# A linear-attention and FFN kernel: all steps of its first part in one table of places, in finer pieces, every place set anew

## Chip, core and metric

The kernel runs on one core of one Trainium2 chip. The metric is the device time in microseconds of one execution, the median over runs.

## What is computed

Two layers follow each other. In the first, each of 8 batches and 8 heads has q, k and v of 576 x 64 (fp32): kv = k^T v, out = q kv, an rms norm over the 64 columns with eps 1e-6, times a gain. The heads are laid side by side, which gives x of 4608 x 512. The second is a feed-forward layer without bias, with the mish function between two products:

```python
kv = np.einsum('bhsd,bhse->bhde', k, v)
out = np.einsum('bhsd,bhde->bhse', q, kv)
x = out / np.sqrt(np.mean(out * out, axis=-1, keepdims=True) + 1e-06) * g_norm
h = x @ w_in            # 4608 x 512 @ 512 x 2048
g = h * np.tanh(softplus(h))
return g @ w_out        # 2048 x 512
```

## The kernel before

The kernel has two parts. The first makes g and writes it to DRAM (gd, gp); the second reads g in blocks of 256 tokens and makes g @ w_out. The change touches the first part, in which w_out is also converted and written to DRAM (wod) for the second.

The 4608 tokens are nine tiles of 512, numbered j. For each tile the attention runs in two units u of four heads, and each unit is a chain of steps (function unit_steps): load (q from DRAM, SP), transpose (PE for tiles 0 and 1, DVE after), project (q times kv, PE), square (ACT), scaled (times the gain, ACT or DVE), sums (PE), rstd (ACT, with two table loads), keep (the rms row to DRAM, SP, line 418), spread (the row back from DRAM, broadcast over 64 partitions, SP, line 424), normalize (DVE, line 432). From tile 1 on the two units share sums, rstd and keep, under unit 1. The steps of kv are k.load (SP), k.mul (PE, line 266), k.keep (ACT).

All products are made in split precision: each operand is a hi half (an ACT copy that rounds, line 115) and a lo half (a DVE subtraction, line 116), and a product is three passes. The FFN of tile 0 is a plain product. From tile 1 on it is a Strassen-like scheme with seven products per 2 x 2 of blocks; the operands made from x are called forms (x_form: A11, S1, S2, S4, A12, S3, A22, in the table numbers 0 to 6), three of which need additions first. Tiles 1 and 2 run alone, tiles 3 to 8 in pairs. The weights have seven forms too; some stay in SBUF, the others are written to DRAM (wid) and streamed back for each group (stream, lines 193 and 194, SP).

The first part is laid out in slots. A slot is one product on PE: 6 matmuls in slots 0 to 31 (line 549), 12 narrow ones in slots 32 to 87 (line 571, slot 34 is empty, slot 90 is one of these), 6 in slots 88 to 255 (line 581). Seven slots are a group. A group opens bank "a" in its first slot; its second-last and last results are added up by DVE in the second, third and fourth slot after it has begun its last two products (line 616), and the last product of a group is made in the third slot of the next group, into the same bank "a", after the addition of block "22" has read it. ACT copies and applies mish to the results (lines 498, 503, 511, 112), GpSimd's queue stores them.

Every other step is put behind a slot by hand: at(t, f) appends f to the list of slot t, and the slot emits first its evictions, then its product, then its list, in the order of the calls. What runs before slot 0 stands in the code as it is emitted. Each engine executes its own instructions in the order of emission. start(j) is the first slot of tile j: 0, 32, 60, 88, 116, 144, 172, 200, 228.

Of the kernel before, what the change touches and what calls it, by code (L numbers as in the profile page):

```python
# [8 lines left out]
F32 = mybir.dt.float32  # L9
# [12 lines left out]
B12 = T4  # L22


@with_exitstack
def linear_attention_rms_mish_ffn(
# [432 lines left out]
    def x_form(j, f, added=False):  # L459
        a11, a12, a21, a22 = x_block(j, 0, 0), x_block(j, 1, 0), x_block(j, 0, 1), x_block(j, 1, 1)  # L460
        xs1 = x_s1(j)
        if f == S1 and not added:
# [5 lines left out]
        split(*x_at(j, f), {A11: a11, S1: xs1, S2: a11, A12: a12, S4: a12, S3: a21, A22: a22}[f])  # L468
# [9 lines left out]
    def at(t, f):  # L478
        plan.setdefault(t, []).append(f)
# [4 lines left out]
    def slot(t, product=None):  # L484
        for f in evict.pop(t, ()):
            f()
        if product:
            product()
        for f in plan.pop(t, ()):
            f()  # L490
# [166 lines left out]
    nc.scalar.preload_act_table_set("natural_log_exp_and_others")  # L657
    weights(0, LOAD)
    rows[0], turned_q = (wfp.tile([P, n, T], F32, name=f"wf{h}4") for n, h in ((TR, "b"), (2, "a")))
    for c in range(TR):  # L660
        rows_load(0, c, 0, 4)
    for name, n in (("k", 2), ("v", 3)):
        kv0[name] = wfp.tile([P, NKC - 1, 9 * D], F32, name=f"wfb{n}")
        kv0[name, NKC] = wfp.tile([P, 9 * D], F32, name=f"pc{n - 2}")
    kv_first(first)
    weights(1, LOAD)
    for c in range(TR):
        rows_load(0, c, 4, 4)
    kv_first(rest)
    for r in (slice(0, D), slice(D, P)):  # L670
        nc.gpsimd.dma_start(gcol[r, :], g_norm.rearrange("(p o) -> p o", o=1))
    weights(2, LOAD)
    weights(3, LOAD)
    make_identity(nc, ident)
    nc.gpsimd.memset(eps, 1e-6)
    nc.gpsimd.memset(ones, 0.0)
    nc.gpsimd.memset(ones[0:D, 0:D], 1.0)
    nc.gpsimd.memset(ones[D:P, D:P], 1.0)
    nc.gpsimd.memset(sel, 0.0)
    for o in range(2):  # L680
        nc.gpsimd.memset(sel[o * D:(o + 1) * D, o:o + 1], 1.0)

    weights(4, LOAD)
    k_load(1, 0)
    k_load(1, 1)

    weights(0, SCALE, JOIN)
    do(0, 0, "transpose", "turned")
    weights(0, BLOCKS)
    kv_first_product(first)  # L690
    kv_first_keep(first)
    weights(1, SCALE)
    do(0, 0, "project", "square")
    weights(1, JOIN)
    do(0, 1, "transpose")
    do(0, 0, "sums")
    do(0, 1, "turned")
    weights(1, BLOCKS)
    do(0, 0, "rstd")
    kv_first_product(rest)  # L700
    kv_first_keep(rest)
    do(0, 0, "normalize")
    do(0, 1, "project")
    weights(2, SCALE)
    x_whole(0)
    do(0, 1, "square")
    weights(3, SCALE)
    rows[1] = att.tile([P, TR, H * D], F32, name="qs")
    for c in range(TR):
        rows_load(1, c, 0, H)  # L710

    def first_slot():
        do(0, 1, "sums")
        weights(2, JOIN)
        do(0, 1, "rstd", "normalize")
# [24 lines left out]
    for b, t, loads, made in (  # L740
        (2, start(0), (21, 22, 23, 28), (27, t1 + 2)),
# [6 lines left out]
        for n in range(2):  # L748
            at(t + made[n], lambda b=b, n=n: k_product(b, n))
            at(t + made[n] + 1, lambda b=b, n=n: k_keep(b, n))  # L750
        for p in range(4):
            at(t + loads[p], lambda b=b, p=p: k_load(b, p))

    def attention(j, t, steps):
        def both():
            units[j][0]["spread"]()
            units[j][1]["spread"]()
        units[j][0]["both"] = both
        for u, n, *names in steps:
            at(t + n, lambda u=u, names=names: do(j, u, *names))  # L760
# [439 lines left out]
```

## Time and profile before

| | us |
|---|---|
| median of 3 runs | 868.23 |
| lowest, highest | 866.71, 868.54 |
| the profiled execution | 872.09 |
| its span, first to last instruction | 870.3 |

The rows below come from the profiled execution; times in them count from the start of its span. In a timeline row the first number is the start, the second the length, and in brackets stands how long the engine was idle before and what ended that. A name such as "ur<-a,ur" is the tile written and the tiles read. "SPq" is SP's queue, whose rows are issues of transfers. PEclk is the granted share of TensorE's clock.

### The profile page before, as it was taken

How to read it: one execution, taken by the hardware profiler on the slowest of the kernel's cores; microseconds unless marked ns; L12 is line 12 of the kernel's file. 1: busy time of each engine (PE TensorE's matmuls, PEld its weight loads, DVE VectorE, ACT ScalarE, POOL GpSimd, SP SyncE). 2: the span in 40 equal slices, each digit the busy share in tenths (PEclk: the TensorE clock that was granted, in tenths of full speed). 3: DMA queues.
4: the chain of work that ended last, by engine and by line, in shares of the span. 5: the costliest groups of instructions: out<-in, count | busy, mean ns of one | idle time of the engine just before them, and what ended most of it. 6: DMA issues, size and time to landing. Idle time of an engine off the chain costs nothing.

```text
span 870.3 us, 14063 instructions
## 1 busy us (share of the span) xinstructions
PE 799.6 (92%) x5456; PEld 666.0 (77%) x5456; DVE 580.8 (67%) x714; ACT 439.2 (50%) x639; POOL 104.1 (12%) x191
## 2 busy tenths in 40 slices
PE   5899899997998669788799999999999999999998
PEld 3677788796766547566688898888888888888887
DVE  3676745556464486454826368888878787888875
ACT  3766663764544354445546565444444445444452
POOL 1010412110222122222111110000000000000000
PEclk9999989998999989899999999999999999999999
DMA  9967887986998947877776764345344333444421
GB/s 279 300 232 249 291 315 237 291 247 216 309 317 287 283 152 244 259 273 248 283 239 237 264 220 158 121 147 168 122 159 132 121 121 121 129 148 131 154 69 49
DMA packets 118434, 181.09 MB, mean 208 GB/s; under 512 B 18720, under 2 KB 80160, under 8 KB 118368
## 3 DMA queue, kind: packets, MB, share of 16 engines
q1 hardware_dynamic: 102848, 128.74, 48.6%
q0 software_dynamic: 15424, 51.39, 15.5%
q8 instruction: 43, 0.70, 0.4%
q14 instruction: 23, 0.19, 0.1%
q10 hardware_dynamic: 96, 0.07, 0.0%
HBM read 119.21 MB, written 60.95 MB: 207 GB/s over the span
## 4 chain that ended last, share of the span: by engine, by line
PE 66%; DMA 15%; DVE 9%; ACT 4%; issue 3%; SPq 3%; POOL 0%; DVEq 0%; ACTq 0%; POOLq 0%
PE a L956 14%; PE bc L956 11%; PE a L581 10%; PE a L961 7%; PE bc L581 7%; PE bc L961 5%; DMA wfa<-wid 3%; DMA qs<-in_q_dram 3%; DMA fa<-rd 2%; PE a L571 2%; DMA wod<-w 2%; PE x L372 1%; PE bc L549 1%; PE a L549 1%; PE bc L571 1%
## 5 line engine op out<-in xcount | busy, mean ns | idle before, releaser
L112 ACT ACTIVATE ur<-ur 128x1024 f32<-128x1024 f32 x32 | 33.9, 1060 | 69.3 <-DVE ur L616 69.3
L581 PE MATMUL a<-pc,wfb 128*128 128x512 f32 x96 | 39.3, 452 | 28.1 <-DVE ur L616 28.1
L616 DVE TENSOR_TENSOR ula<-bc,ula 128x512 f32<-128x512 f32 x32 | 22.0, 688 | 62.9 <-PE bc L581 35.9
L581 PEld LDWEIGHTS a<-pc,wfb 128*128 128x128 f32 x96 | 20.7, 216 | 37.6 <-DVE ur L616 32.4
L581 PE MATMUL bc<-wfa,wfa 128*128 128x512 f32 x144 | 37.8, 399 | 7.9 <-DMA wfa<-wid 7.2
L581 PEld LDWEIGHTS bc<-wfa,wfa 128*128 128x128 f32 x144 | 26.8, 189 | 15.0 <-DVE wx L121 4.0
L511 ACT COPY ur<-a 128x512 f32<-128x512 f32 x32 | 18.8, 588 | 37.9 <-PE a L581 30.0
L581 PE MATMUL a<-wfc,wfc 128*128 128x512 f32 x96 | 37.3, 430 | 0.0
L581 PE MATMUL bc<-wfc,wfb 128*128 128x512 f32 x144 | 37.2, 394 | 0.0
L581 PE MATMUL a<-wfa,wfb 128*128 128x512 f32 x144 | 36.9, 392 | 0.0
L116 DVE TENSOR_TENSOR wfa<-g,wfa 128x1024 fp32r<-128x1024 f32 (+1 forms) x24 | 27.5, 1155 | 12.8 <-ACT wfa L115 12.8
L115 ACT CAST wfc<-wfb 128x1024 fp32r<-128x1024 f32 x23 | 24.0, 1051 | 20.9 <-PE a L961 7.8
L581 PE MATMUL bc<-pa,wfb 128*128 128x512 f32 x96 | 34.0, 395 | 0.0
L581 PE MATMUL a<-pb,wfa 128*128 128x512 f32 x96 | 33.6, 390 | 0.0
L115 ACT CAST wfa<-g 128x1024 fp32r<-128x1024 f32 (+1 forms) x24 | 23.8, 998 | 18.7 <-PE a L961 7.8
L581 PEld LDWEIGHTS bc<-wfc,wfb 128*128 128x128 f32 x144 | 27.3, 191 | 6.3 <-issue 0.3
L581 PEld LDWEIGHTS a<-wfa,wfb 128*128 128x128 f32 x144 | 26.7, 188 | 6.6 <-issue 1.0
L112 ACT ACTIVATE ula<-ula 128x512 f32<-128x512 f32 x32 | 20.2, 632 | 21.7 <-DVE ula L616 21.7
L115 ACT CAST wfa<-wfb 128x1024 fp32r<-128x1024 f32 x19 | 19.9, 1051 | 21.5 <-PE a L961 15.5
L116 DVE TENSOR_TENSOR wfa<-wfb,wfa 128x1024 fp32r<-128x1024 f32 x19 | 23.1, 1221 | 8.9 <-ACT wfa L115 8.9
L616 DVE TENSOR_TENSOR ur<-bc,ur 128x512 f32<-128x512 f32 x32 | 21.9, 683 | 10.5 <-PE bc L581 3.6
L1011 DVE TENSOR_TENSOR ur<-ow 128x1024 f32<-128x1024 f32 x16 | 19.6, 1224 | 13.1 <-ACT ow L1008 13.1
(516 smaller groups left out, 2460.1 us busy)
## 6 DMA issues: line engine op xcount, KB each, us to landing
gp<-ur POOLq DMA_DIRECT2D x24, 512.0 KB, 5.2
g<-gp SPq DMA_DIRECT2D x12, 1024.0 KB
wfb<-gp SPq DMA_DIRECT2D x12, 1024.0 KB
wfa<-wid SPq DMA_DIRECT2D x18, 512.0 KB
w<-in_moe_w_out_dram SPq DMA_DIRECT2D x32, 256.0 KB
km<-in_k_dram SPq DMA_DIRECT2D x28, 288.0 KB
vm<-in_v_dram SPq DMA_DIRECT2D x28, 288.0 KB
gp<-ula POOLq DMA_DIRECT2D x24, 256.0 KB, 4.2
```

The costliest lines, as they stand in the source:

```text
L112: nc.scalar.activation(o, i, AF.Mish)
L115: nc.scalar.copy(hi, src)
L116: nc.vector.tensor_sub(lo, src, hi.bitcast(F32))
L372: nc.tensor.matmul(st["x"][a][half(o), c], kv[r], st["q"][r, a, c], start=True, stop=True)
L511: then(t + 4, lambda: nc.scalar.copy(dst(st, "12"), st["a"]))
L549: nc.tensor.matmul(banks[m], w[:, a, kc, :], xf[b][:, kc], start=r == kc == s == 0, stop=(r == kc == 1 and s == 2), skip_group_check=True,)
L571: nc.tensor.matmul(bank[:, jj * TH:(jj + 1) * TH], w[:, a, kc, :], xf[b][:, kc], start=first and jj == kc == s == 0, stop=(kc == 1 and s = ...
L581: nc.tensor.matmul(bank, w[:, a, kc, :], xf[b][:, kc], start=first and kc == s == 0, stop=(kc == 1 and s == 2), skip_group_check=True,)
L616: nc.vector.tensor_add(o, bank_view(st, block, bank), o)
L956: nc.tensor.matmul(bank.rearrange("p (s h n) -> p s h n", s=2, h=2), gf[0][:, c], wo_form(c, right), start=first and c == 0, stop=False, s ...
L961: nc.tensor.matmul(halves(bank)[:, 0], gf[1][:, c], wo_form(c, right)[:, 0], start=False, stop=c == NF2 - 1, skip_group_check=True)
L1011: nc.vector.tensor_add(st["o"].rearrange("p r (c n) -> p (r c) n", c=2), a[:, :, 0], a[:, :, 1])
```

## The change

A table WHEN gives each of 485 steps of the first part a place, a number with three decimals; its whole part is the slot, and within a slot the steps are sorted by place. Steps before slot 0 have negative places. The finer pieces: a form is now its addition (f{j}.{f}.sum, DVE), its hi half (f{j}.{f}.0, ACT) and its lo half (f{j}.{f}.1, DVE), each with a place; the two spreads of a tile, each step of a unit, each step of a weight block (w{j}) and of a chunk of w_out (o{i}), the streams (s{i}.{n}), the loads and splits of the second part's weights (p{c}) and its early forms (e{c}.{f}) have one each. Instructions, transfers and tiles are the same; order and place differ. The diff, cut:

```diff
+WHEN = {
+    "w1.load": -57.761, "w1.scale": -57.665, "kv.a": -56.646, "rows.a": -56.517, "w0.load": -55.073, "kv.mul.a": -54.701,
...
+    "x0.1.square": -11.17, "x0.1.sums": -9.952, "w2.scale": -8.597, "w2.join": -6.356, "x0.1.rstd": -5.266,
...
+    "w2.blocks": -2.398, "w3.scale": -1.588, "k1.load2": 1.685, "k1.mul0": 2.528, "k1.keep0": 4.733, "w3.join": 5.805,
...
+    "k3.load0": 29.125, "x2.1.load": 29.175, "f1.0.1": 30.119, "w4.diff": 30.214, "k2.mul1": 30.411, "f1.2.sum": 30.523,
...
+    "x2.0.square": 31.886, "k3.load1": 31.947, "f1.4.0": 32.101, "f1.2.0": 32.737, "f1.4.1": 32.792, "f1.2.1": 33.196,
...
+    "x2.0.scaled": 39.667, "x2.1.project": 40.062, "x3.0.load": 40.076, "w5.sums": 40.306, "k3.mul0": 40.507,
...
+    "w4.store": 49.281, "x2.1.rstd": 49.741, "x2.1.keep": 50.313, "k3.keep1": 50.903, "x3.0.transpose": 51.079,
+    "w6.store": 51.568, "k4.load1": 51.698, "k4.mul0": 52.246, "w7.sums": 52.262, "x2.0.spread": 52.367,
+    "x2.0.normalize": 52.723, "x3.0.project": 52.826, "x2.1.spread": 53.018, "f2.0.0": 53.224, "pools.xt": 54.093,
...
+    "x3.1.normalize": 71.16, "x4.1.sums": 71.188, "x4.1.rstd": 72.176, "pools.wx": 72.928, "x4.1.scaled": 72.948,
+    "o0.load": 73.332, "o0.scale": 73.59, "x5.0.load": 73.996, "x4.1.keep": 74.235, "x3.0.spread": 74.587,
+    "o0.join": 75.149, "f3.4.0": 75.377, "x3.0.normalize": 75.565, "f3.0.0": 75.727, "x4.1.spread": 76.127,
...
+    "o0.store": 79.406, "x4.0.spread": 79.7, "x4.1.normalize": 80.724, "x4.0.normalize": 81.317, "k5.keep0": 81.319,
+    "k5.load3": 81.38, "k6.load0": 81.631, "k5.mul1": 82.565, "k6.load1": 82.703, "k5.keep1": 83.056, "f3.1.sum": 84.967,
+    "f3.2.sum": 85.423, "f3.1.0": 85.515, "x5.1.load": 85.681, "k6.load2": 85.804, "f3.2.0": 86.314, "f3.1.1": 86.495,
...
+    "x5.1.scaled": 103.717, "o4.load": 104.024, "x5.0.spread": 105.109, "s0.2": 105.184, "x5.1.spread": 105.458,
...
+    "k7.keep1": 122.327, "x6.1.sums": 122.642, "o6.load": 123.413, "x6.1.rstd": 123.617, "x6.1.keep": 124.487,
+    "s0.5": 124.541, "o6.scale": 126.126, "x6.0.spread": 126.594, "o6.join": 127.287, "o6.diff": 127.431,
+    "o6.store": 128.496, "x6.0.normalize": 131.613, "x6.1.spread": 132.132, "x7.0.transpose": 132.458, "o7.load": 133.0,
+    "x6.1.normalize": 133.011, "f5.1.sum": 133.652, "o7.scale": 134.666, "o7.join": 136.841, "f5.0.0": 137.267,
...
+    "o9.scale": 154.219, "o9.join": 155.712, "o10.load": 156.204, "o9.diff": 157.661, "x7.0.spread": 157.999,
+    "x7.0.normalize": 158.323, "x8.0.transpose": 158.502, "o9.store": 158.999, "o10.scale": 159.093, "s1.2": 160.404,
...
+    "o13.load": 176.057, "o13.scale": 176.556, "x8.1.rstd": 176.69, "o13.join": 176.923, "s1.4": 178.899,
+    "o13.diff": 179.328, "o13.store": 179.491, "o14.load": 180.623, "o14.scale": 181.143, "o14.join": 183.595,
+    "x8.1.keep": 183.886, "s1.5": 184.157, "o14.diff": 184.314, "o14.store": 184.554, "x8.0.spread": 185.555,
+    "x8.0.normalize": 186.509, "o15.load": 187.081, "x8.1.spread": 187.181, "x8.1.scaled": 188.636, "o15.scale": 189.095,
+    "o15.join": 190.662, "s1.6": 191.845, "x8.1.normalize": 193.314, "f7.1.sum": 193.614, "f7.0.0": 194.153,
+    "f7.0.1": 194.91, "f7.1.0": 197.56, "f7.2.sum": 197.819, "f7.1.1": 198.895, "f7.4.0": 199.888, "f7.2.0": 200.459,
...
+    "s2.4": 231.214, "p3.load": 232.696, "p2.load": 233.51, "e0.6": 234.071, "p1.split": 235.921, "p4.load": 236.909,
...
+    "e1.1": 249.971, "p5.load": 250.354, "p5.split": 250.686, "e1.0": 254.85,
+}
...
-    def x_form(j, f, added=False):
...
+    def x_sum(j, f):
+        a11, a12 = x_block(j, 0, 0), x_block(j, 1, 0)
+        if f == S1:
             x_add(j)
         elif f == S2:
-            nc.vector.tensor_sub(a11, xs1, a11)
+            nc.vector.tensor_sub(a11, x_s1(j), a11)
         elif f == S4:
             nc.vector.tensor_sub(a12, a12, a11)
...
+    def x_form(j, f, low):
...
+        if low:
+            nc.vector.tensor_sub(lo, src, hi.bitcast(F32))
+        else:
+            nc.scalar.copy(hi, src)
...
     def at(t, f):
-        plan.setdefault(t, []).append(f)
+        plan.setdefault(int(t // 1), []).append((t, f))
+
+    def step(name, t, f):
+        at(WHEN.get(name, t), f)
...
+    def steps(t):
+        for _, f in sorted(plan.pop(t, ()), key=lambda s: s[0]):
             f()
...
+    for t in sorted(t for t in plan if t < 0):
+        steps(t)
```

The places of the same steps before, where the text speaks of them: k3.load0 and k3.load1 32 and 35, k3.mul0 41, w7.sums 48, k4.load1 51, x2.1.rstd 49, x2's spreads 52 and normalizes 56 and 57, x3's spreads 72 and normalizes 76 and 77, x4's spreads 79 and normalizes 83 and 84, s0.2 102, x6's rstd 128, spreads 131 and normalizes 135 and 136, x7's spreads 163 and normalizes 167 and 168, x8.0.transpose 164, s1.4 172 (after o14.load, also 172), x8's spreads 187 and normalizes 191 and 192, p5.load 250 and p5.split 258. A hi half was directly followed by its lo half.

## Rows read from the trace of the kernel before

**Rows 1.** The page of the profiled execution, its first part: each engine's busy us, share of the span, and instructions.

```profile
PE 799.6 (92%) x5456; PEld 666.0 (77%) x5456; DVE 580.8 (67%) x714; ACT 439.2 (50%) x639; POOL 104.1 (12%) x191
```

**Rows 2.** Busy time of each engine in stretches that begin at the first matmul of slots 0, 32, 60, 88, 116, 144, 172, 200, 228 and 256. The columns: the stretch, its length, then for each engine the busy us and the number of instructions, the granted clock, the busy share of the 16 DMA engines, and what they moved in GB/s.

```profile
0.00:27.04 27.04, 15.73 (x181) 9.96 (x181) 10.17 (x11) 13.34 (x17) 2.68 (x15) 1.00 0.99 294
27.04:88.15 61.11, 58.22 (x469) 42.74 (x469) 43.88 (x58) 39.55 (x61) 6.52 (x12) 1.00 0.82 253
88.15:143.95 55.80, 50.03 (x580) 46.34 (x581) 31.12 (x50) 31.44 (x57) 16.84 (x29) 0.94 0.89 302
143.95:201.01 57.06, 53.99 (x706) 47.92 (x705) 34.49 (x41) 33.71 (x53) 7.94 (x12) 1.00 0.84 255
201.01:255.15 54.14, 48.24 (x376) 36.64 (x375) 29.17 (x40) 27.71 (x43) 10.54 (x18) 0.94 0.81 268
255.15:314.59 59.44, 46.69 (x337) 35.41 (x336) 33.09 (x51) 25.78 (x40) 15.59 (x27) 0.94 0.86 276
314.59:376.45 61.86, 48.94 (x218) 35.84 (x217) 36.86 (x57) 29.33 (x43) 15.59 (x27) 0.89 0.75 236
376.45:425.93 49.48, 43.57 (x186) 32.44 (x185) 28.93 (x44) 24.19 (x35) 13.77 (x24) 0.97 0.82 282
425.93:472.11 46.18, 41.21 (x170) 33.22 (x169) 24.13 (x32) 25.77 (x40) 6.60 (x13) 0.93 0.62 218
472.11:512.70 40.59, 40.59 (x191) 34.04 (x189) 18.69 (x34) 22.41 (x42) 6.92 (x13) 1.00 0.64 222
512.70:870.32 357.62, 352.35 (x2059) 311.41 (x2057) 290.27 (x303) 166.00 (x215) 1.08 (x2) 1.00 0.42 133
```

**Rows 3.** The timeline of PE: the matmuls in front of which PE stood for 1.5 us or more between slot 0 and slot 256. They are in slots 41, 90, 117, 124, 139, 146, 160, 167, 174, 180 and 202.

```profile
110.41 0.37 PE L266 MATMUL ss<-vm,km 64*64 64x64 f32 x2 [4.18 <-DMA vm<-in_v_dram]
...
210.79 2.93 PE L571 MATMUL a<-pd,wfb 128*128 128x256 f32 x12 [5.62 <-DVE ur L616]
...
259.45 1.63 PE L581 MATMUL bc<-wfa,wfa 128*128 128x512 f32 x6 [1.57 <-DMA wfa<-wid]
...
272.53 1.62 PE L581 MATMUL bc<-wfa,wfa 128*128 128x512 f32 x6 [2.03 <-DMA wfa<-wid]
...
305.82 0.79 PE L581 MATMUL a<-pc,wfb 128*128 128x512 f32 x1 [7.52 <-DVE ur L616]
...
325.31 0.79 PE L581 MATMUL a<-pc,wfb 128*128 128x512 f32 x1 [6.58 <-DVE ur L616]
...
352.21 0.50 PE L581 MATMUL a<-pc,wfb 128*128 128x512 f32 x1 [2.98 <-DVE ur L616]
...
365.71 0.80 PE L581 MATMUL a<-pc,wfb 128*128 128x512 f32 x1 [3.36 <-DVE ur L616]
...
380.85 0.50 PE L581 MATMUL a<-pc,wfb 128*128 128x512 f32 x1 [1.52 <-DVE ur L616]
...
394.31 2.22 PE L581 MATMUL bc<-wfa,wfa 128*128 128x512 f32 x6 [3.57 <-DMA wfa<-wid]
...
434.07 0.80 PE L581 MATMUL a<-pc,wfb 128*128 128x512 f32 x1 [4.20 <-DVE ur L616]
```

**Rows 4.** The chain of work that ended last, in order of time: two consecutive slots each (start, length, count of matmuls).

```profile
325.31 5.29 PE a L581 x12
...
434.07 5.49 PE a L581 x12
...
474.99 2.72 PE a L581 x12
```

**Rows 5.** The timeline of DVE ahead of slots 139 and 202, with the addition of line 616 that PE waited for (305.08), and an instruction of a join of w_out, a form's first addition and lo halves (lines 122, 456, 116) for their lengths.

```profile
299.98 1.23 DVE L432 TENSOR_TENSOR wfa<-wfa,fh 128x1024 f32<-128x1024 f32 x1 [6.34 <-DMA fh<-rd]
...
302.15 1.23 DVE L432 TENSOR_TENSOR wfa<-wfa,fa 128x1024 f32<-128x1024 f32 x1 [0.34 <-DMA fa<-rd]
...
303.75 0.69 DVE L122 SCALAR_TENSOR_TENSOR wx<-w,wx 128x512 uint32<-128x512 uint32 x1
...
305.08 0.68 DVE L616 TENSOR_TENSOR ur<-a,ur 128x512 f32<-128x512 f32 x1
...
306.84 1.18 DVE L456 TENSOR_TENSOR s<-wfa,wfa 128x1024 f32<-128x1024 f32 x1
...
426.33 1.23 DVE L116 TENSOR_TENSOR pa<-x,wfc 128x1024 fp32r<-128x1024 f32 x1 [1.12 <-ACT wfc L115]
...
432.19 1.23 DVE L116 TENSOR_TENSOR pb<-x,pa 128x1024 fp32r<-128x1024 f32 x1 [1.17 <-ACT pa L115]
```

**Rows 6.** The timelines of SP's queue (issues) and of DVE: three spreads (the third normalize is the last DVE row), and a load of w_out chunks in front of a streamed weight.

```profile
133.33 1.96 SPq L424 DMA_DIRECT2D fh<-rd  x2
...
140.17 1.23 DVE L432 TENSOR_TENSOR x<-x,fh 128x1024 f32<-128x1024 f32 x1 [4.26 <-DMA fh<-rd]
...
290.88 1.28 SPq L424 DMA_DIRECT2D fh<-rd  x2
...
361.55 1.26 SPq L424 DMA_DIRECT2D fh<-rd  x2
...
367.02 1.23 DVE L432 TENSOR_TENSOR x<-x,fh 128x1024 f32<-128x1024 f32 x1 [0.38 <-DMA fh<-rd]
...
375.98 10.65 SPq L135 DMA_DIRECT2D w<-in_moe_w_out_dram  x4
386.73 0.58 SPq L193 DMA_DIRECT2D wfa<-wid  x1
```

More of the change, by code (lines that the diff above doesn't have):

```diff
@@ L683, in linear_attention_rms_mish_ffn @@
[L683 to L703, printed above, removed]
@@ new lines, in constants, with gains @@
+    def constants():
+        make_identity(nc, ident)
+        nc.gpsimd.memset(eps, 1e-6)
+        nc.gpsimd.memset(ones, 0.0)
+        nc.gpsimd.memset(ones[0:D, 0:D], 1.0)
+        nc.gpsimd.memset(ones[D:P, D:P], 1.0)
+        nc.gpsimd.memset(sel, 0.0)
+        for o in range(2):
+            nc.gpsimd.memset(sel[o * D:(o + 1) * D, o:o + 1], 1.0)
+    def gains():
+        for r in (slice(0, D), slice(D, P)):
+            nc.gpsimd.dma_start(gcol[r, :], g_norm.rearrange("(p o) -> p o", o=1))
@@ new lines, in linear_attention_rms_mish_ffn @@
+    turned_q = None
+    t1 = start(1)
+    begin = (
+        ("table.exp", lambda: nc.scalar.preload_act_table_set("natural_log_exp_and_others")),
+        ("w0.load", None), ("rows.a", rows_first), ("kv.a", kv_rooms), ("w1.load", None), ("rows.b", rows_second),
+        ("kv.b", lambda: kv_first(rest)), ("gains", gains), ("w2.load", None), ("w3.load", None), ("constants", constants),
+        ("w4.load", None), ("k1.load0", None), ("k1.load1", None),
+        ("w0.scale", None), ("w0.join", None), ("x0.0.transpose", None), ("x0.0.turned", None), ("w0.blocks", None),
+        ("kv.mul.a", lambda: kv_first_product(first)), ("kv.keep.a", lambda: kv_first_keep(first)),
+        ("w1.scale", None), ("x0.0.project", None), ("x0.0.square", None), ("w1.join", None),
+        ("x0.1.transpose", None), ("x0.0.sums", None), ("x0.1.turned", None), ("w1.blocks", None),
+        ("x0.0.rstd", None), ("kv.mul.b", lambda: kv_first_product(rest)), ("kv.keep.b", lambda: kv_first_keep(rest)),
+        ("x0.0.normalize", None), ("x0.1.project", None), ("w2.scale", None), ("whole.0", lambda: x_whole(0)),
+        ("x0.1.square", None), ("w3.scale", None), ("rows.c", rows_next),
+    )
@@ new lines, in linear_attention_rms_mish_ffn @@
+    early = {name: n - len(begin) for n, (name, _) in enumerate(begin)}
+    for name, f in begin:
+        if f:
+            step(name, early[name], f)
+    for n, (name, f) in enumerate((
+        ("x0.1.sums", lambda: do(0, 1, "sums")), ("w2.join", lambda: weights(2, JOIN)), ("x0.1.rstd", lambda: do(0, 1, "rstd")),
+        ("x0.1.normalize", lambda: do(0, 1, "normalize")), ("whole.1", lambda: x_whole(1)), ("w2.blocks", lambda: weights(2, BLOCKS)),
+        ("table.mish", lambda: nc.scalar.preload_act_table_set("mish")),
+    )):
+        step(name, 0.01 + 0.01 * n, f)
@@ L1047, in linear_attention_rms_mish_ffn @@
     ):
-        at(t8 + n, lambda f=f, c=c: early_form(f, c))
+        step(f"e{c}.{f}", t8 + n, lambda f=f, c=c: early_form(f, c))
+    for i in range((NT - SINGLE) // 2):
+        order = [(6 - 2 * i + n) % NF2 for n in range(NF2)]
+        for n in range(1, NF2 - 1):
+            step(f"s{i}.{n}", start(SINGLE + 2 * i) + 7 * n, lambda j=order[n + 1], n=n: stream(j, (n + 1) % 2))
+    for t in sorted(t for t in plan if t < 0):
+        steps(t)
     prev = None
```

150 lines of the change are left out of this document (61 added, 89 removed), and 61 rows, old and new, of the table WHEN.

## The prediction

> **What bounds the kernel now.** The page comes first, for the engines' shares [rows 1]: TensorE (PE) is busy 92%, so the question is where the other 8% lies. The second view cuts the span at the first matmul of slots 0, 32, 60, 88 and so on [rows 2]. The last stretch, which this change does not touch, has 357.6 us with PE busy for 352.4. In the 485.7 us from 27.04 to 512.70 PE is idle for 54.2 (length less busy time, stretch by stretch: 2.9, 5.8, 3.1, 5.9, 12.8, 12.9, 5.9, 5.0, 0.0). The stretch without idle time shows what a slot costs when nothing is late: 2.72 us for two [rows 4], 1.36 each, and 1.44 in the slots of line 571.
>
> The idle time is not spread out. The PE timeline shows eleven waits that hold 43.1 us of it [rows 3], and three kinds of releaser. Seven end with the VectorE (DVE) addition of line 616, the one that must read bank "a" before the next group's third slot adds to it. Three end with a streamed weight (wid), one with a k/v load. After the long ones the clock is at the lower of its two levels (1.2 instead of 2.4 GHz): the granted clock is 0.89 in the stretch with most of them and 1.00 in the one without [rows 2], and the 12 matmuls behind two of them took 5.29 and 5.49 us instead of 2.72 [rows 4], so a long wait costs 2.6 us more.
>
> Why is the addition late? Not from load: DVE is busy 36.9 of 61.9 us in the worst stretch [rows 2]. Its queue is in order, and the DVE timeline [rows 5] shows two things in front of the addition. At 299.98 and 302.15 it stands for a normalize whose rms row is still on its way from DRAM. At 426.33 and 432.19 it stands 1.12 and 1.17 us each time for ScalarE (ACT), because hi and lo halves of a form follow each other immediately. Similarly the queue of SP: the stream issued at 386.73 stood behind a load of w_out that took from 375.98 to 386.63 to get its room [rows 6].
>
> **The change part by part.** No instruction's work, transfer or buffer changes; only the orders of the engines' queues do. So each cost is a wait, and the sum goes stretch by stretch. I compare the table's order on each queue with the old one. Only the order on a queue counts: a queue runs ahead of PE's slots wherever its waits allow, so many of the new places change nothing.
>
> Start and slots 0 to 31: the transfers fill the first 27.04 us (share 0.99), the bytes in front of the first product stay the same, and the longest chain is reshuffled. Against it, x0.1.sums now precedes slot 0 and k1.mul0 slot 3. I take 0; the ends are a gain of 2.9 us (the idle time of the second stretch) and a loss of 4.2 (one wait for a k/v load, as at 110.41 [rows 3]).
>
> Slots 32 to 59: k3.load0 and k3.load1 go from 32 and 35 to 29 and 32, ahead of k3.mul0 at the same slot; the wait of 4.18 and its 2.6 go (6.8). But x2.0.normalize moves from place 56 to 52.7, in front of the addition of slot 53, which slot 55 needs. Its spread was issued at 133.33 and read at 140.17 [rows 6]; with w7.sums on ACT and k4.load1 on SP now behind the rstd and the keep that lead to it, I put it 2 us earlier. The addition then ends near 140, slot 55 was ready at 136.8: 3.3 us and a half clock of 2.6. Net gain 1.
>
> Slots 60 to 87: small waits now, 3.1 us. x3.0.spread moves behind o0.load, x5.0.load and x4.1.keep on SP, x4's normalizes come earlier. I take 0, ends a gain of 3.1 and a loss of 4.
>
> Slots 88 to 115: the wait at 210.79 (5.62 and 2.6). The table starts f3.1.sum at the same place, but gives each hi half to ACT well before the lo half: DVE has 2.44 + 4 x 1.22 + 2 x 0.68 = 8.7 us in front of the addition (durations from [rows 5]), against five slots of 1.44, 7.2. That leaves 1.5. s0.2 comes behind o4.load (place 104), which waits for a store: another 1.5. With 0.7 for the rest, 3.7 of 8.2 stay: gain 4.5.
>
> Slots 116 to 143: the stream waits at 259.45 and 272.53 go (s0.3 and s0.4 no longer stand behind a blocked w_out load). The wait at 305.82: x6's rstd moves from 128 to 123.6, 4.4 slots or 6.0 us. Slot 139 was ready at 298.3, the second normalize could run at 302.15, now at 296.2 by the slots; behind it stand the normalize, two additions of a form, a join of w_out (three instructions of at most 0.69) and three additions of results, 1.23 + 2.44 + 1.8 + 3 x 0.68 = 7.5 us to the end of the one that counts [rows 5]. So at most 5.4 stay, less what SP's shorter queue brings; I take 2.7 and a half clock. 12.8 + 2.6 - 5.3: gain 10.
>
> Slots 144 to 171: at 325.31 the same ping-pong of halves as above; 6.58, 2.98, 3.36 and two half clocks. x8.0.transpose no longer stands between. What comes instead: x7.0.normalize at 158.3 behind an x7.0.spread at 158.0, itself behind o10.load on SP, which waits for o8.store. DVE stands there and has 6.6 us of work queued before the addition that slot 166 needs. I leave 5 of 18.1: gain 13.
>
> Slots 172 to 199: s1.4 goes ahead of o14.load on SP, and the 3.57 at 394.31 with its slow matmuls ends; the 1.52 at 380.85 too. Gain 6.
>
> Slots 200 to 227: in front of the addition before slot 202 now stand 1.23 + 2.44 + 3 x 1.22 + 2 x 0.68 = 8.7 us of DVE from place 193.3, done near 199.7 in slots. The 4.20 and 2.6 go, 1 stays: gain 6.5.
>
> Slots 228 to 256: no idle now. p1 to p4 load 9 to 23 slots later and p5.split directly follows p5.load, so ACT stands for a transfer in front of the last evictions. I take a loss of 2, ends 0 and 6. The part behind keeps its 357.6.
>
> Sum 0 + 1 + 0 + 4.5 + 10 + 13 + 6 + 6.5 - 2 = 39. Against it stands what I cannot place. The transfers' busy share times length, stretch by stretch, is 411 us of the 512.7 [rows 2]; the same bytes in 40 us less means a share of 0.87 instead of 0.80. In the two stretches with shares of 0.86 and 0.89 PE now idles 16% of the time, in the last two before 512.70 (0.62 and 0.64) 6%. I charge 9 us, between 0 and half the gain. Forecast: 30 us. The profiled execution took 872.09 (span 870.3) against a median of 868.23, a ratio of 0.9956; 842 becomes 838.
>
> **A rule weighed against the rows.** The spreads took from issue to the normalize that waited 6.8, 9.1 (290.88 to 299.98) and 5.5 us (361.55 to 367.02) [rows 5, 6]. The Trainium skill, page "DMA: Bandwidth & Descriptors", section "Anatomy of one DMA — SWDGE (gpsimd) path", gives about 2.0 us plus bytes at 436 GB/s, for these 256 KB an estimate of 2.6 us; it is stated for the other issuing path, and this trace disagrees by a factor of two or more.
>
> **The rivals.** *Normalize stalls take the gain (slower).* Eight normalizes (x2.0, x2.1, x3.1, x3.0, x4.0, x6.1, x7.0, x8.0) lie 0.3 to 1.6 places behind their spread; before, 4 or 5. If SP reaches those spreads no sooner than their place, each holds DVE for 5.5 to 9.1 us less about 1.4. PE has some two slots of slack (2.8), so each brings a gap of 1.3 to 4.9 and a half clock of 2.6: 31 to 60 us against 39 gained. It decides from 4.9 us each; at 7 each the time is 872 + 17, or 885. For it: SP also stands in front of stores that must land. Against: in the old order too SP got ahead of its places wherever it was free. Chance 0.16.
>
> *The moves are mostly no moves.* SP and PE already set the pace, the order on each queue matters little, and the waits move. Then 868, within 0.2%, which is about what a measurement of this kernel can tell from no change. Against: the forms' hi and lo halves do change order. Chance 0.04.
>
> *The transfers take half.* In the stretches with a share over 0.85 the idle time stays (12.8 + 5.8 and their clock); gain 10 to 18, so 851 to 860. Chance 0.20.
>
> *All listed waits go and nothing comes.* 39 + 10 of those I left standing: 872 - 49 is 823, or 820. It needs spreads that land before their normalize everywhere; the 5.5 to 9.1 us of the rows speak against it. Chance 0.10. By the estimate of 2.6 us from the Trainium skill's page named above, this case would be the result.
>
> **How the numbers follow.** The forecast, 825 to 850, has 0.50; its own time is 838. Faster by over 0.2%: 0.50 + 0.20 + 0.10 = 0.80; same 0.04; slower 0.16. The range leaves out half of the best case and most of the slower one: 819 to 872.
>
> **What would show it.** Right: in the new trace the waits at slots 42, 90, 139, 146, 160, 167, 180 and 202 are gone or under 3 us; slot 256 starts near 482; the stretch behind it keeps its 358; the lo halves on DVE no longer wait 1.1 us for ACT. New waits I expect at slots 55, 110, 139 and 166, each led by line 432 on DVE or by wid. Wrong: normalizes that stand over 5 us with PE gaps behind; idle time spread over stream loads with shares near 1; or a longer last stretch because p-loads come late.

## The result: 818.77 us

The changed kernel takes 818.77 us (median of 4 runs, 816.75 to 819.21) against 867.91 for the kernel before (866.71 to 868.54): a ratio of 0.9431, 95% interval 0.9411 to 0.945, 49 us faster. The forecast was 838, the range 819 to 872: the time lies 0.2 us below it. Three of the medians below leave out one far longer execution each (981.38, 1558.37 and 1429.11 us). The profiled execution took 819.2 (span 817.4) where that of before took 872.09: 52.9 us.

The page after, its first part, answers to [rows 1]: the same 5456 matmuls take 17.7 us less. ACT has two instructions more, 641 against 639: loads of a function table of 1.28 us each, which the new order brings (20 against 18).

```profile
PE 781.9 (96%) x5456; PEld 660.7 (81%) x5456; DVE 578.5 (71%) x714; ACT 441.6 (54%) x641; POOL 104.0 (13%) x191
```

The stretches between the first matmuls of the same slots, with the columns of [rows 2]:

```profile
0.00:30.48 30.48, 16.21 (x184) 10.94 (x185) 12.55 (x14) 15.35 (x19) 2.62 (x15) 1.00 0.96 292
30.48:87.97 57.49, 57.49 (x554) 43.99 (x553) 46.48 (x63) 42.45 (x65) 10.28 (x19) 1.00 0.93 287
87.97:138.35 50.38, 47.83 (x581) 44.90 (x580) 30.78 (x50) 31.19 (x58) 12.56 (x21) 0.97 0.93 311
138.35:197.22 58.87, 54.93 (x707) 49.95 (x705) 36.20 (x44) 36.65 (x55) 11.11 (x18) 0.94 0.95 290
197.22:242.48 45.26, 44.50 (x362) 34.93 (x359) 23.80 (x36) 24.53 (x39) 11.61 (x20) 1.00 0.97 315
242.48:293.34 50.86, 45.28 (x281) 34.30 (x280) 35.09 (x52) 26.25 (x39) 12.75 (x23) 0.97 0.86 283
293.34:341.55 48.21, 44.48 (x201) 33.09 (x200) 31.73 (x48) 26.68 (x38) 14.71 (x26) 0.96 0.85 272
341.55:383.01 41.46, 40.94 (x185) 31.70 (x184) 29.06 (x44) 25.20 (x37) 12.46 (x22) 1.00 0.89 312
383.01:421.09 38.08, 38.08 (x169) 31.54 (x168) 19.18 (x31) 20.45 (x33) 8.30 (x15) 1.00 0.73 256
421.09:461.69 40.60, 40.60 (x191) 34.05 (x190) 25.27 (x40) 28.35 (x50) 6.50 (x12) 1.00 0.77 268
461.69:817.40 355.71, 351.58 (x2059) 311.26 (x2057) 288.40 (x300) 164.53 (x212) 1.08 (x2) 1.00 0.43 134
```

Read beside [rows 2], the gains by stretch are: start and slots 0 to 31 together 0.2 (slot 0 comes 3.4 us later, the stretch behind it is 3.6 shorter), then 5.4, -1.8, 8.9, 8.6, 13.7, 8.0, 8.1, 0 and, in the second part, 1.9. PE's idle time between slots 0 and 256 falls from 54.2 to 17.1 us (length less busy). Its busy time in the same slots falls from 431.5 to 414.1, and the clock column accounts for most of that: 0.89 to 0.97 in six stretches before, 0.96 to 1.00 in the same ones after (in slots 60 to 87 it went the other way, 1.00 to 0.94). An estimate from these rows, length times what the clock lacks to 1.00 summed over the stretches, is 21.7 us before and 8.5 after, so 13 of the 17.4. So 37.1 us of waits took 17.4 us of matmul time with them, and the later start gives 3.4 back: 51.0. The second part's 1.9 makes it 52.9.

What went is the view that groups PE's waits by what ended them (total us, times, longest). Before, three kinds hold 41.8 us and a k/v load 5.0:

```profile
PE a L581 <- DVE ur L616: 28.1, 9, 7.5
...
PE bc L581 <- DMA wfa<-wid: 7.2, 3, 3.6
PE a L571 <- DVE ur L616: 6.5, 2, 5.6
PE ss L266 <- DMA vm<-in_v_dram: 5.0, 2, 4.2
```

After, there is no wait of bank "a" for the addition at all (34.6 us before), that of bank "bc" is 3.6 (0.8 before), and stream and k/v loads have lost 7.0 of 12.2. The first row stands ahead of slot 0 and belongs to the later start:

```profile
PE s L351 <- DMA wfb<-in_v_dram: 11.1, 1, 11.1
PE bc L680 <- ACT ur L612: 3.9, 1, 3.9
PE bc L690 <- DVE ula L725: 3.6, 1, 3.6
PE a L690 <- ACT ula L607: 3.4, 1, 3.4
PE bc L690 <- DMA wfa<-wid: 2.7, 2, 1.9
PE ss L362 <- DMA vm<-in_v_dram: 2.5, 1, 2.5
```

(Lines 571, 581, 616 of before are 680, 690, 725 now; 266, 498 and 503 are 362, 607 and 612; 115 and 116 of a form are 571 and 569, 432 is 528, 424 is 520.) The PE timeline has six waits of over 0.5 us between slots 32 and 256, in slots 52, 79, 110, 117, 138 and 168; none stands where one of [rows 3] stood, but for slot 117:

```profile
124.57 0.27 PE L362 MATMUL ss<-vm,km 64*64 64x64 f32 x2 [2.55 <-DMA vm<-in_v_dram]
...
178.05 0.58 PE L680 MATMUL bc<-pc,wfb 128*128 128x256 f32 x1 [3.94 <-ACT ur L612]
...
234.20 0.47 PE L690 MATMUL bc<-wfa,wfa 128*128 128x512 f32 x1 [0.76 <-DMA wfa<-wid]
...
247.65 0.72 PE L690 MATMUL bc<-wfa,wfa 128*128 128x512 f32 x2 [3.64 <-DVE ula L725]
...
283.83 0.47 PE L690 MATMUL bc<-wfa,wfa 128*128 128x512 f32 x1 [1.93 <-DMA wfa<-wid]
...
334.67 0.80 PE L690 MATMUL a<-wfc,wfc 128*128 128x512 f32 x1 [3.38 <-ACT ula L607]
```

The one of slot 79, followed back: the copy that PE waits for stands on ACT behind a hi half, that behind a normalize on DVE, that behind a spread, which SP issued at 170.16 (ACT's timeline, then DVE's, then SP's):

```profile
176.47 1.04 ACT L571 CAST wfa<-x 128x1024 fp32r<-128x1024 f32 x1 [7.19 <-DVE x L528]
177.42 0.58 ACT L612 COPY ur<-bc 128x512 f32<-128x512 f32 x1
```

```profile
175.21 1.23 DVE L528 TENSOR_TENSOR x<-x,fh 128x1024 f32<-128x1024 f32 x1 [6.49 <-DMA fh<-rd]
```

```profile
170.16 1.27 SPq L520 DMA_DIRECT2D fh<-rd  x2
```

The one of slot 168 has the same form: a first pass over a w_out chunk stands on ACT until the buffer that it writes has been stored, and the copy for bank "a" stands behind it.

```profile
332.01 0.66 ACT L222 ACTIVATE wx<-w 128x512 f32<-128x512 f32 x1 [9.05 <-DMA wod<-wx]
...
334.04 0.57 ACT L607 COPY ula<-a 128x512 f32<-128x512 f32 x1
```

So has the one of slot 117, on DVE: a transpose stands 4.96 us for a transfer, and the addition for bank "bc" behind it.

```profile
243.98 1.25 DVE L446 STREAM_TRANSPOSE fl<-qs 128x1024 f32<-128x1024 f32 x1 [4.96 <-DMA wfa<-wid]
...
246.91 0.68 DVE L725 TENSOR_TENSOR ula<-bc,ula 128x512 f32<-128x512 f32 x1
```

### The profile page after: what moved, and what is told of

Read it like the earlier page. It is cut to its first block, busy times and chain, and to the rows that moved or that the text cites. A ratio compares the mean times of both kernels' runs of the same rounds, so it can differ in the third digit from the quotient of the medians.

```text
span 817.4 us, 14052 instructions
## 1 busy us (share of the span) xinstructions
PE 781.9 (96%) x5456; PEld 660.7 (81%) x5456; DVE 578.5 (71%) x714; ACT 441.6 (54%) x641; POOL 104.0 (13%) x191
## 4 chain that ended last, share of the span: by engine, by line
PE 80%; DMA 9%; issue 5%; ACT 2%; SPq 1%; DVE 1%; POOL 1%; ACTq 0%; POOLq 0%; DVEq 0%
PE a L1061 15%; PE bc L1061 11%; PE a L690 10%; PE a L1066 8%; PE bc L690 7%; PE bc L1066 6%; PE a L680 5%; PE bc L680 3%; PE a L658 3%; PE q L1209 2%; PE bc L658 2%; PE x L468 2%; DMA wod<-wx 2%; DMA qs<-in_q_dram 2%; DMA wfa<-wid 2%
## 5 line engine op out<-in xcount | busy, mean ns | idle before, releaser
L690 PE MATMUL a<-wfc,wfc 128*128 128x512 f32 x96 | 34.9, 405 | 3.7 <-ACT ula L607 3.4
L690 PE MATMUL a<-wfa,wfb 128*128 128x512 f32 x144 | 37.1, 393 | 0.0
L690 PE MATMUL a<-pc,wfb 128*128 128x512 f32 x96 | 33.9, 393 | 0.0
L725 DVE TENSOR_TENSOR ur<-a,ur 128x512 f32<-128x512 f32 x32 | 21.9, 685 | 11.8 <-PE a L690 8.1
L211 ACT CAST wfc<-g 128x1024 fp32r<-128x1024 f32 x17 | 17.7, 1051 | 17.2 <-PE a L1066 11.7
```

The lines of the kernel that those rows point to most:

```text
L211: nc.scalar.copy(hi, src)
L690: nc.tensor.matmul(bank, w[:, a, kc, :], xf[b][:, kc], start=first and kc == s == 0, stop=(kc == 1 and s == 2), skip_group_check=True,)
L725: nc.vector.tensor_add(o, bank_view(st, block, bank), o)
```

## The experiments

Each kernel ran beside the kernel before on the same chip, whose median in these groups of runs was 865.8 to 867.9. The changed kernel itself was not run again in these groups: a difference from it compares medians of two groups, and by the ratios to the kernel before it comes out up to 3 us different. "Back" means that a family of steps gets its old place again, the order within a slot kept. In the families f are the forms, x the attention, o the chunks of w_out, s the streams, k the k/v steps.

**Families put back, one at a time.**

```diff
+WHEN.update({
+    "f1.0.0": 28.007, "f1.0.1": 28.009, "f1.1.sum": 30.001, "f1.1.0": 30.003, "f1.1.1": 30.005, "f1.2.sum": 31.001,
...
+})
```

> The new kernel, with the places that the forms (additions, hi halves, lo halves) had before the change; everything else at its new place. Theory (in-order waits on DVE and ACT ahead of the line of result additions were the loss, and the forms' halves are one half of them): the waits at slots 90, 146 and 202 come back in part, 5.6 + 6.6 + 4.2 us and a half clock of 2.6 each, less what the earlier normalizes save of them: 10 to 20 us slower than the new kernel, 829 to 839. Rival (the gain is that of SP's queue, earlier loads and an even stream of transfers): 818 to 822, since no transfer moves.

In this kernel one addition of the forms of tiles 7 and 8 reads rows that are not yet normalized. Measured: 844.22 (ratio 0.9751, 0.9687 to 0.9815), 25 us lost of the 49. That is above the theory's range; the rival falls.

```diff
+WHEN.update({
+    "x5.0.load": 72.007, "x5.0.transpose": 81.001, "x5.1.load": 82.001, "x5.0.project": 88.001,
...
+})
```

> The new kernel, with the attention steps of tiles 5 to 8 and the forms of tiles 5 and 7 at their places before the change; the chunks of w_out, the streams, k/v and all of tiles 0 to 4 keep the new ones. Theory (normalizes that stand for their row, and forms, ahead of the result additions): the waits at slots 139, 146, 160, 167 and 202 come back, 24.6 us and some 10 of half clock, so 20 to 35 us slower than the new kernel, 839 to 854. Rival (SP's queue and the spread of the w_out chunks made the gain): the chunks keep their places, so under 8 us, 819 to 827.

Here three products of tiles 5 and 6 read the kv of the next batch. Measured: 846.96 (0.977, 0.9715 to 0.9825), 28 lost, inside the theory's range.

```diff
+WHEN.update({
+    "o0.load": 93.003, "o0.scale": 101.003, "o0.join": 101.005, "o0.diff": 102.003, "o0.store": 103.005,
...
+})
```

> The new kernel, with the chunks of w_out (load, scale, join, differences, store) and the streamed weights at their places before the change. Theory: the three stream waits come back (1.6 + 2.0 + 3.6 us and some 2.6 of half clock) and chunks stand in front of some additions: 8 to 16 us slower than the new kernel, 827 to 835. Rival (spreading the chunks over the transfers is the main gain): 25 us and more, 844 and above.

Measured: 855.91 (0.989, 0.9835 to 0.9945), 37 lost: the family that I held for the cheapest costs the most. The size is the rival's, and the theory's mechanism did not come: not one wait for a streamed weight is in PE's waits of this run. The three losses sum to 91 of 49 us; the first two share the forms of tiles 5 and 7, but forms and w_out with streams share no step and come to 62. Each of the three brought bank "a"'s waits for the addition back (11.2, 10.0 and 13.2 us in PE's waits by what ended them; none in the changed kernel), and the rest of each loss stands in other waits. Families cannot be priced one by one, which the next group tests from the other side.

**Everything back, and one family alone.** The first kernel has the finer pieces and the table, with all 485 places old; the other three have one family's new places on that.

```diff
+WHEN.update({
+    "table.exp": -0.99, "w0.load": -0.97, "rows.a": -0.95, "kv.a": -0.93, "w1.load": -0.91, "rows.b": -0.89,
...
+})
```

> The changed kernel's finer steps and its one table, with every place put back to that of the kernel before (order within a slot kept). Theory (the gain is all in the places): within 4 us of the kernel before, 864 to 872, with the eleven waits of the kernel before back. Rival (the finer pieces or the code around them bring something by themselves): 860 or less.

Measured: 865.03 (0.998, 0.9949 to 1.0011): the pieces and the table bring nothing; the places bring all of it. Of the eleven waits of [rows 3], though, only six are in its profiled execution (slots 42, 90, 146, 160, 167 and 202). The 7.52 us of slot 139 are not, and slots 116 to 143 take 53.25 us where they took 59.44 (columns as in [rows 2]):

```profile
254.96:308.21 53.25, 47.96 (x337) 35.68 (x336) 31.79 (x50) 24.46 (x39) 15.82 (x27) 0.94 0.89 293
```

So the list of waits is in part that of the one execution that was profiled, or of small differences in how this kernel is emitted; the runs don't tell which. The gains by stretch above carry that uncertainty, those of slots 116 to 143 above all.

> The other way round from the run that put w_out and the stream pages back: on the old places of all else, only the w_out steps (o) and the stream pages (s) have their new places (the first three w_out sets squeezed behind slot 88, where the buffers of the old order allow them). Theory (the orders of the families fit one another, so that a family put back does more harm than it does good alone): 860 to 872, a gain of at most 8. Rival (the families' gains add, so that this one is worth the 37 us that its going back cost): 840 or less.

Measured: 863.71 (0.9954, 0.9933 to 0.9976), a gain of 4, as the theory has it.

> On the old places of all else, only the forms of the tile pairs from 3 on have their new places (four of them moved by up to 3 slots to stay behind the normalizing that they read). The third of the families by itself. Theory (the orders fit one another; 4 us gained by w_out and stream alone, 25 lost by the attention alone): 855 to 880, so that the three families by themselves bring nothing or a loss in sum, against 49 together. Rival (the forms are what carries the gain): 845 or less.

Measured: 855.89 (0.9876, 0.9826 to 0.9927), a gain of 10; the rival falls.

> On the old places of all else, only the steps of the attention of tiles 3 to 8 (loads, transposes, products, sums, spreads, normalizing) have their new places; one addition of the forms of tiles 7 and 8 is moved 0.4 slots to stay behind the normalizing that it reads. Theory (as before, the orders fit one another): 850 to 866, a gain of 2 to 18, with waits left at the slots of the forms and of w_out (90, 146, 160, 167, 180, 202). Rival (the attention alone carries the gain, as the weight of its waits in the kernel before suggests): 840 or less.

Measured: 893.35 (1.0285, 1.0254 to 1.0316): 25 us slower than the kernel before. The rival falls, and the theory had not allowed for a loss either. Sum of the three alone: 4 + 10 - 25 = -11. The steps outside the three families (weights, k/v, tiles 1 and 2, the second part's loads) never ran alone, so what they bring by themselves is open. PE's waits in that kernel show where the early attention does harm while forms and chunks stay, above all at the additions and at a transpose.

```profile
PE a L766 <- DVE ur L801: 20.6, 7, 11.1
PE x L544 <- DVE fl L522: 11.3, 2, 8.9
```

**The transfers.** Fourteen copies of 0.59 MB more, or 6.9 MB less, in both kernels.

```diff
+    def more_transfers():
+        for n in range(14):
+            spare_dram = tc.dram_tile([P, 1152], F32, name=f"xd{n}")
...
+            at(92.5 + 8 * n, lambda t=spare_dram, src=src: nc.gpsimd.dma_start(t, src))
```

> The new kernel with 14 more transfers of 0.59 MB each, DRAM to DRAM, issued on GpSimd's queue at places 92.5, 100.5 and so on to 196.5; nothing reads what they write. At the 302 GB/s of the busiest stretch before the change that is 27 us of transfer time in slots 92 to 200. Theory (the first part still has room in its transfers there, and my charge of 9 us for them was the wrong step): 0 to 5 us slower, 819 to 824. Rival (transfers already set the pace of these slots): 14 us or more, since every added us of transfer is then on the path, 833 to 846, with waits that end with wid and qs.

Measured: 829.49 (0.9572, 0.9511 to 0.9634), 10.7 more than the changed kernel: between the two, and against the theory's 0 to 5. From 197 to 293 us, about slots 88 to 144, the transfers had a share of 0.99 and 1.01 (columns as in [rows 2]), and still some 16 of the 27 us added were hidden:

```profile
197.00:242.00 45.00, 41.84 (x411) 32.28 (x402) 24.96 (x38) 22.92 (x36) 11.96 (x21) 0.92 0.99 323
242.00:293.00 51.00, 47.44 (x296) 36.33 (x295) 32.11 (x49) 26.11 (x42) 15.66 (x28) 1.00 1.01 344
```

> The kernel before with the same 14 extra copies of 0.59 MB from DRAM to DRAM in slots 92 to 196 that cost the changed kernel 10.7 us. My sum charged 9 us for the transfers' share going up from 0.80 to 0.87. If the charge was right in kind (a fuller queue costs more), the same copies cost the kernel before, with its emptier stretches, clearly less: 0 to 5 us, 868 to 873. Rival (each transfer costs by where it lands, not by how full the engines are): 8 to 14 us, 876 to 882, as in the changed kernel.

Measured: 874.31 (1.0089, 1.0052 to 1.0127), 8.6 more than the kernel before: the rival's size, not the theory's.

```diff
-            st["w"] = load_words(pools["w64"].tile([P, 4, P, 2], U32, name="w64"), srcs, 1)
+            i = 2 * c + h
+            if i < 2:
+                kept[i] = pools["w64"].tile([P, 4, P, 2], U32, name="w64")
+            st["w"] = load_words(kept[i % 2], srcs, 1, P if i < 2 else 8)
```

> The changed kernel with less to transfer: of the sixteen sets of w_out the last fourteen load 8 of their 128 rows instead of all, into the tile that an earlier set left, so 6.9 MB less (about 23 us of transfer time at the 294 GB/s of the first stretch) with the same instructions on every engine's queue; w_out's products are then not those of the reference. Theory (the transfers do hold the changed kernel up, so that a charge was right in kind and was only made up for elsewhere): 6 to 14 us faster, 805 to 813. Rival (they are hidden, and the charge was wrong in kind): 816 to 820.

Measured: 810.73 (0.9358, 0.9315 to 0.9401), 8.0 less, inside the theory's range. Most of it is one wait, 5.0 of the 5.6 us between the profiled spans: in slots 144 to 171 (48.21 us above) the pass that stood on ACT for 9.05 us no longer holds up slot 168.

```profile
293.14:336.32 43.18, 42.80 (x201) 32.15 (x200) 31.88 (x48) 25.90 (x37) 14.88 (x26) 1.00 0.82 256
```

> The kernel before with the same fourteen loads cut (part of the computation left out as in the run before). Theory (a fuller queue costs more): clearly less gain than in the changed kernel, 0 to 5 us, 862 to 867. Rival (transfers cost the same wherever the order is in-order and tight): the same gain as in the changed kernel, 6 to 14.

Measured: 858.64 (0.991, 0.9883 to 0.9937), 8.5 less. So the same transfers cost the two kernels about the same (10.7 and 8.6 when added, 8.0 and 8.5 when taken away), some 0.3 to 0.4 us for each us of transfer time at 294 GB/s (8.26 MB are 28 us, 6.9 MB 23). The intervals leave a difference of 4 to 6 us either way open. Both forecasts of the theory of a dearer fuller queue were missed.

**The waits that are left.** Three sets of new places, each aimed at the waits of the run before it. The core of the first, and of the second:

```diff
+    "k4.mul0": 55.6, "x3.0.spread": 72.94, "f3.0.0": 76.2, "x6.1.transpose": 114.9, "o4.join": 115.2,
+    "o4.diff": 116.3, "o4.store": 116.4, "o11.scale": 167.6, "o11.join": 167.62, "o11.diff": 167.64,
+    "o11.store": 167.9, "s0.6": 132.95, "o7.scale": 136.5, "o7.join": 137.3, "s0.2": 103.9,
...
+    "o0.scale": 75.2, "o0.join": 75.6, "k5.mul1": 84.05, "k5.keep1": 85.02, "x2.0.normalize": 53.1, "f2.0.0": 53.3,
+    "f2.3.0": 62.9, "f2.3.1": 63.6, "s0.3": 112.0, "k7.load3": 114.2, "k7.mul1": 119.1, "x8.1.project": 173.3,
+    "o12.scale": 172.2, "o13.scale": 178.1, "o13.join": 178.3,
```

> The changed kernel with fourteen places set anew, for the six waits that its TensorE still has in slots 52, 79, 110, 117, 138 and 168 (2.55, 3.94, 0.76, 3.64, 1.93 and 3.38 us, sum 16.2). The product of k that stood in slot 52 goes to slot 55; the spread that slot 79's form needs goes ahead of two loads on SP, and the form behind slot 76's evictions; the transpose and the halves of w_out behind slot 114's to 116's additions; o11's three passes behind slot 168's copy; the loads of the sixth and second stream pages ahead of the w_out loads that stood before them, with o7's passes later. Theory (these waits are the heads of in-order queues, each standing before work that was ready, and an order without them exists): the profiled span falls by 10 to 17 us, time 802 to 809, the six waits gone or under 1 us, no new one above 2. Rival (the transfers of these stretches, busy 0.93 to 0.97, are what is short, and each wait comes back under another name): 814 or more.

Measured: 819.42 (0.9444, 0.9414 to 0.9475), nothing gained: the rival's time. The waits of slots 52, 79, 110, 138 and 168 are gone, and at slot 117 the addition no longer holds PE, but a streamed weight does, 2.04 us instead of 3.64. So the heads were what held these slots; but with that one nine waits stand in the trace (16.1 us). Slots 88 to 171 are 8.7 us shorter, slots 60 to 87 and 172 to 199 10.3 longer.

> The first set of new places again, with fifteen more for the nine waits that came in that run, in slots 55, 65, 77, 82, 117 (two), 172, 180 and 182 (1.65, 0.94, 2.22, 3.34, 2.04, 1.83, 2.07, 1.51 and 0.50 us, 16.1 in all): each step that stood at the head of its queue goes behind the next eviction or product, the sixth stream page and one k/v load go earlier on SP. Theory (the waits are only a matter of order, and the second round finishes what the first began): 801 to 810, no wait of over 1.5 us left between slots 32 and 256. Rival (the transfers of the first part, whose 16 engines are busy 0.91 to 0.97 of the time up to slot 144, have no room left, and the waits go round): 814 to 820, with waits of 10 us or more in sum under new names.

Measured: 817.22 (0.9434, 0.9386 to 0.9482), the rival's time. The profiled execution is the fastest of its five, 811.74, with 13.4 us of waits left, nine of the thirteen under 1.2 us. The five scatter from 811.7 to 823.4, over 11 us against 2.5 in the changed kernel, and the median has gained 1.6, less than its interval.

> The new places of the second set, but in slots 60 to 87 those of the changed kernel (that stretch got longer by 4.8 and 3.3 us in the first and second set), and four stream pages of the second tile pair (to slots 168, 176, 182 and 189) ahead of the w_out load that stood before each on SP. Theory (each stretch has its own best order, and the gains of the others stay): slots 60 to 87 take 59 us again, slots 172 to 199 42 to 43, the profiled span is 803 to 809, the median 806 to 813. Rival (with transfers busy over 0.9 of the time what one stretch gains the next one gives back): median 815 to 820 and the stretch at slot 60 still over 61 us.

Measured: 816.94 (0.9406, 0.9365 to 0.9448): inside the rival's 815 to 820, and with the rival's sign: the stretch from slot 60 to 88, with the changed kernel's own places, takes 63.25 us, not 59. The wait of slot 79 is back in it, and longer: the spread ahead of it took 7.9 us from issue (169.08) to normalize (176.93).

```profile
179.77 0.58 PE L687 MATMUL bc<-pc,wfb 128*128 128x256 f32 x1 [6.25 <-ACT ur L619]
```

The three sets' rows of that stretch (columns as in [rows 2]; first set, second, third):

```profile
135.92:199.61 63.69, 57.19 (x706) 51.59 (x705) 36.22 (x44) 36.55 (x55) 11.13 (x18) 0.92 0.91 279
```

```profile
134.32:196.46 62.14, 55.05 (x706) 49.85 (x704) 37.48 (x45) 37.24 (x59) 11.70 (x18) 0.97 0.94 278
```

```profile
135.21:198.46 63.25, 55.07 (x706) 49.60 (x704) 36.53 (x45) 36.71 (x58) 11.71 (x18) 0.95 0.92 280
```

PE arrives 2.4 to 4.0 us earlier than in the changed kernel (138.35), and slot 88 starts at 196.46 to 199.61 in all three (197.22 there): what is gained ahead of this stretch is lost again in it, in the third set for the most part at slot 79.

> The second set of new places with the same fourteen loads cut (part of the computation left out as before). Theory (the transfers make the waits of the new sets come back): 15 us or more below the second set's 817.9, 790 to 803. Rival (the orders themselves do): 810 or more, the stretch from slot 60 to 88 still over 61 us.

Measured: 809.18 (0.9342, 0.9312 to 0.9372), 8.0 below the second set, a little under the rival's 810. That is what the same cut brought the other two kernels, and the theory wanted 15 or more; the stretch from slot 60 takes 59.4 us, 2.7 less, where the rival wanted it over 61:

```profile
135.06:194.46 59.40, 55.24 (x706) 49.74 (x704) 37.61 (x46) 37.39 (x58) 11.74 (x18) 0.97 0.94 293
```

So neither reading holds whole: transfers are a part of why the waits come back, and with fewer of them slot 88 starts at 194.46. Which steps hold it near 197 in the three sets was followed back for the third alone.

## Why the prediction fell short

The sign, the kind of the gain and the slots were right, the size was not: 19 us too little. On the profiled executions the forecast was 872.09 - 30 = 842, measured 819.2. The 22.9 us between them are two errors, 9.0 and 13.9.

**The charge for the transfers: 9 us, of which no run shows anything.** The first step that failed is the one that put a price on what I could not place: a share of 0.87 instead of 0.80 should cost "between 0 and half the gain". The rows behind it were picked: in [rows 2] the stretch that idles most, 12.9 of 61.86 us or 21%, has a share of 0.75, and the one with 0.84 idles 5%. The share did rise, to 0.85 to 0.97 from slot 32 to 200. But the gains by stretch sum to 52.9 without a charge, and fall short of the forecast in two stretches only, by 1.8 and 1.4; the stretch with share 0.97 has a granted clock of 1.00 and 0.8 us of idle time. Transfers do cost: the two runs on the changed kernel went against the reading that they are hidden (10.7 where it had 0 to 5, 8.0 where it had at most 3). They cost the old order about as much, though, so a price that rises with the share is not seen, as far as the intervals reach. That the price was already in the waits of [rows 3] and in those that I left standing, and that I counted it twice, fits this and was not tested by itself.

**What I left standing: the sum of 39, measured 52.9.** By stretch, measured less forecast: +0.2 at the start, +4.4 (slots 32 to 59), -1.8 (60 to 87), +4.4 (88 to 115), -1.4 (116 to 143), +0.7 (144 to 171), +2.0, +1.6, +2.0 (to slot 256), +1.9 in the second part. Two terms carry 8.8 of the 13.9, and in both I had placed a step of DVE too late.

In slots 32 to 59 I put the spread of x2.0 2 us earlier, and with that a wait of 3.3 and a half clock at slot 55. It was issued 13.5 us earlier than before (133.33) and read 13.0 earlier (140.17). The addition behind it ended at 129.0, and slot 55, itself 5.6 us earlier than before, began at 131.15 without a wait; slot 52 stood 2.55 for a k/v load instead.

```profile
119.81 1.27 SPq L520 DMA_DIRECT2D fh<-rd  x2
```

```profile
127.19 1.23 DVE L528 TENSOR_TENSOR x<-x,fh 128x1024 f32<-128x1024 f32 x1 [4.52 <-DMA fh<-rd]
```

In slots 88 to 115 I left 3.7 of 8.2, from 8.7 us of DVE work against five slots of 7.2. The work in front of the addition is just those 8.7 us in the trace, but it began at 185.43, 14.6 us ahead of slot 90 (200.07), and DVE even stood 3.26 us for PE in the middle of it. DVE had run ahead of its places, which the prediction allows in general ("a queue runs ahead of PE's slots wherever its waits allow") and left out of this term.

```profile
185.43 1.22 DVE L552 TENSOR_TENSOR s<-wfa,wfa 128x1024 f32<-128x1024 f32 x1
...
197.04 0.69 DVE L725 TENSOR_TENSOR ur<-a,ur 128x512 f32<-128x512 f32 x1
```

Of the waits that I named for new ones (55, 110, 139, 166) only that of slot 110 came, 0.76 of the 1.5; p5.split held up nothing (2 forecast). The five others came at slots that I had not named. Three of them (79, 117, 168) have the mechanism that I had, a step at the head of DVE's or ACT's queue that stands for a transfer. In slots 52 and 138 PE stood for its own operand, a k/v load and a streamed weight that took 12.8 us from issue (271.05) to the product (283.83).

Smaller slips of the sum: in slots 200 to 227, 4.20 + 2.6 - 1 is 5.8 and not 6.5; a gain of 10 to 18 is a time of 850 to 858 and not 851 to 860; 823 times 0.9956 is 819.4 and not 820.

**The rival of the normalizes: its premise came in part, its price did not.** DVE stood longer for spreads than before. The idle time of DVE in front of line 432, before:

```profile
  DMA fh<-rd: 15.3, 6
  DMA fa<-rd: 6.9, 6
```

and in front of line 528, after:

```profile
  DMA fh<-rd: 17.7, 5
  DMA fa<-rd: 12.4, 5
```

That is 30.1 us in 10 waits against 22.2 in 12, 3.0 us each against 1.9, and less than the 4.1 to 7.7 that the rival had for each. I had priced each with a gap of 1.3 to 4.9 on PE. One of the ten has such a gap behind it, slot 79's 3.94, with 6.49 us on DVE; this is the sign that I had named for being wrong, once. No wait of PE leads back to one of the other nine. So the new places changed less how long DVE stands than what stands behind it.

The attention's places by themselves, on the old order, come to 893.35, near the rival's 885, but that is luck and not its mechanism. Of some 60 us of PE's waits in that run, 7.5 end right behind a normalize (6.29 and 1.22). The 6.29 stood for the addition behind this one:

```profile
316.94 1.22 DVE L604 TENSOR_TENSOR wfa<-wfa,fa 128x1024 f32<-128x1024 f32 x1 [6.14 <-DMA fa<-rd]
```

Its two longest, 11.07 and 8.86, have other things in front: lo halves that stood for ACT and transposes that stood 2.87 and 4.68 for q.

**The case that came** is the one to which I gave 0.10, "all listed waits go and nothing comes", 820. Its time came by luck: 17.1 us of idle time are left, new waits came, and its condition failed, for the spreads did not land in the 2.6 us estimated from the Trainium skill, page "DMA: Bandwidth & Descriptors", section "Anatomy of one DMA — SWDGE (gpsimd) path". A spread is two transfers of 256 KB and not one (x2 in its row), for which the same formula gives an estimate of 3.2 us. The one of slot 79 took 5.05 us from issue (170.16) to the normalize (175.21), a little under the 5.5 to 9.1 of [rows 5, 6]; the trace of after disagrees with the formula as that of before did. **The rest**: that the lo halves follow their hi halves later was right; that slot 256 comes near 482 was wrong by 20 (461.69), all of it ahead of that slot.

## What to carry to other kernels

In an order that is written out for in-order queues, a step's cost is what stands behind it while it waits, so the same steps moved alone can cost 25 us and together with the rest save 49: price an order as a whole, and look for the first instruction behind each stalled one that the bounding engine needs. When you place a step, ask when its queue can reach it, not at which place it stands: two terms here were wrong by over 4 us each for that. Before you charge for a busier transfer queue on top of the waits, add the same transfers to both versions and compare. When the listed waits go and the time stays (819, 817, 817 here), look for the waits that came in their place: 13 to 18 us stood in each of these three.

## What the runs showed of the hardware

The transfer engines ran at a share of 0.99 to 1.01 for 96 us (323 and 344 GB/s) in the run with more copies, and PE idled only 6.7 us of them. Without the copies PE idles 6.3 us in slots 88 to 143, at shares of 0.97 and 0.86. And a wait has a price beside its length: in this change 37.1 us of waits fewer came with 17.4 us of matmul time fewer, at a granted clock of 0.96 to 1.00 in the six stretches where it had been 0.89 to 0.97.
